# A last product split over two PSUM banks, and a copy moved behind an exponential

## The chip, the cores and the metric

The kernel runs on one core of one Trainium2 chip. The metric is the device time of one execution in microseconds. The core's engines are TensorE (PE; its weight loads are shown as PEld), VectorE (DVE), ScalarE (ACT), GpSimd (POOL) and SyncE (SP), and 16 DMA engines move data. Each engine runs its own instructions in order, and engines wait for each other by semaphores.

## The reference

Two layers are chained. The first is attention over 8 batches of 8 heads, 576 positions of 64 values each, with sparse masks: heads 0 to 3 are local (a position sees the 32 last ones up to itself), heads 4 to 7 are strided (a position sees the earlier ones with the same remainder by 32).

```
scores = scale * np.matmul(q, k.transpose(0, 1, 3, 2))
masks  = local for h < 4: 0 <= i - j < 32;  strided for h >= 4: j <= i and j % 32 == i % 32
attn   = softmax(where(masks, scores, -1e9))
x      = np.matmul(attn, v), heads side by side: 4608 tokens x 512
```

The second layer is a projection of the 4608 tokens to 2048 values, a leaky activation with a slope per column, and a projection back to 512:

```
h = x @ w_in
g = np.maximum(h, 0.0) + alpha * np.minimum(h, 0.0)
out = g @ w_out
```

Inputs and output are 32 bit floats; inside, the kernel uses 16 bit floats for the operands of matmuls.

## The kernel before

**The loop.** The tokens are cut into nine chunks of 512. The loop over n = 1 to 8 does chunk n's second layer in 30 steps: 16 steps of `lin1_piece` (L624 matmuls into a PSUM tile hps, ACT's `neg` at L636, DVE's combination into gT at L638) and 14 of `fast_piece`. `fast_piece` computes the projection back by a scheme of seven products of half-size blocks (P1, P4, P2, P6, P5, P7, P3, in this order), each in two halves of eight matmuls (L693). Their sums collect in four PSUM accumulators X, Y, Z and V: Y begins as a copy of X behind P1 (`seed`, L719), V as a copy of Y behind P6, and P3 adds onto V. DVE adds the accumulators onto output tiles (L644, through `sub`), and SP stores them.

**The attention in between.** Between these steps `attn_n` takes pieces of the attention of batch n + 1 from a list that was made ahead. A pair is two heads (four pairs to a batch, the last two strided), and a pair's work is one score piece (L411 matmuls, exponentials on ACT, masks on DVE), two or three pv pieces (L454 matmuls, L461 and L463 on DVE), and the turning of its result into xT, the input of `lin1_piece`. The score piece makes two halves. The first half's exponential (L424) and mask (L426) are issued at once. The second half's exponential is two instructions (L430), put into the list `defer`, and one is issued after each following step.

**The turning.** For batches from the third on, the first three pairs of a batch are turned by a DMA: `x_dma` issues it on SP. For the third pair, the first strided one, it writes a tile xs (L486), and ACT then copies xs into xT in token order (`x_copy`, L493, 128x576). The fourth pair is turned by eight transposes on TensorE into a PSUM tile xp (L471) and copied by ACT (L207). Of the list's iteration g, the score piece is that of pair g, the pv pieces those of pair g - 1, the transposes those of pair g - 2, and `x_copy` that of pair g - 3. So `x_copy` stands at the start of the next batch's second iteration, which is also where the loop over n goes on to its next chunk.

**PSUM.** Two pools of three one-bank tiles each: `phpool` (hps and the accumulators) and `pspool` (second halves of scores, pv, xp, and each third hps); a third pool holds the first half of the scores. A tile that is allocated again waits until the former one has been read.

**The end.** In the last chunk P3's two halves are added and stored apart, each 128 rows by 256 columns, so that the first store can start before the second half is done. Both halves lie in the same accumulator tile V:

Of the kernel before, what the change touches and what calls it, by code (L numbers as in the profile page):

```python
# [9 lines left out]
F32 = mybir.dt.float32  # L10
F16 = mybir.dt.float16
ALU = mybir.AluOpType
# [19 lines left out]
def kernel(  # L32
# [10 lines left out]
    nc = tc.nc  # L43
    keep = tc.keep_in_program_order
# [48 lines left out]
    pspool = ctx.enter_context(tc.tile_pool(name="ps", bufs=3, space=bass.MemoryType.PSUM))  # L93
    phpool = ctx.enter_context(tc.tile_pool(name="ph", bufs=3, space=bass.MemoryType.PSUM))
# [5 lines left out]
            name=nc.get_next_instruction_name(), act_func_set_id=6, ins=[], outs=[]  # L100
# [17 lines left out]
    DX = 2  # L118
# [184 lines left out]
    def turn_rows(b, nm):  # L303

        dst = qTs[0][:, :, 0:576] if nm == "q" else kTs[0][:, :, 32:608]
        for e in range(2):
            keep(nc.sync.dma_start_transpose(
                dst[:, e].rearrange("r (t p) -> r t p", p=96),
                rowed[(b, nm)][0:96, 768 * e : 768 * e + 768]))
# [187 lines left out]
    npair = 4 * B  # L497
    pairs = [make_pair(g) for g in range(npair)]
    pieces = []

    def feed(fn, g):
        pieces.append((g, fn))

    def T(u, nm):
        return lambda: transpose_piece(u, nm)

    def Pv(g, i):
        return lambda: pv_piece(pairs[g], i)

    def X(g):  # L510
        return lambda: x_piece(pairs[g])

    for g in range(7, npair + 2):
        c = g // 4
        a, p, t = g, g - 1, g + 1
        okA = 8 <= a < npair
        okP = 8 <= p < npair
        okT = 8 <= t < 4 * LX and t % 4 == 0
        nP = len(pairs[p].pgroups) if okP else 0
        seq = []  # L520
        if okA:
            seq.append(("S", lambda a=a: score_both(pairs[a])))
        if okP:
            seq.append(("P", Pv(p, 0)))
        if okT:
            seq.append(("T", T(t // 2, "q")))
        if 8 <= g - 2 < npair and not pairs[g - 2].xd:
            seq.append(("X", X(g - 2)))
        if okP:
            seq.append(("P", Pv(p, 1)))  # L530
        if okT:
            seq.append(("Tk", T(t // 2, "k")))
        if nP == 3:
            seq.append(("P", Pv(p, 2)))
        if not seq:
            seq.append(("N", lambda: None))

        todo = [(c, pr) for pr in range(2)] if g % 4 == 0 and 8 < g < npair else []

        if g % 4 == 1 and 9 <= g and c + 1 < B:  # L540
            todo = [(c + 1, nm) for nm in "qk"]
        lastP = max([i for i, z in enumerate(seq) if z[0] == "P"], default=len(seq) - 1)
        nslots = [i for i, z in enumerate(seq) if z[0][0] != "S"] or list(range(len(seq)))
        for i, (kind, fn) in enumerate(seq):
            extra = []
            if todo and i in nslots:
                left = len([z for z in nslots if z >= i])
                cnt = -(-len(todo) // max(1, left))
                extra = [todo.pop(0) for _ in range(min(cnt, len(todo)))]

            def run(fn=fn, extra=extra, g=g, c=c, kind=kind, lastp=(i == lastP), first=(i == 0)):
                fn()
                if first and g % 4 == 2 and LX <= c + 1 < B:
                    turn_rows(c + 1, "q")
                    turn_rows(c + 1, "k")
                for b, pr in extra:
                    if pr in ("q", "k"):
                        if b < LX:
                            cast_l(b, pr, "act")
                        if b + 1 < LX:  # L560
                            load_qk(b + 1, False, pr)
                        continue
                    cast_v(b, pr, "act" if b >= LX else "dve")
                    if pr == 1 and b + 1 < B:
                        load_v(b + 1, True)
                if kind == "Tk" and g % 4 == 3 and c + 3 < LX:
                    load_tail(c + 3, False)
                if lastp and g % 4 == 3 and LX <= c + 2 < B:
                    load_rows(c + 2, "q")
                    load_rows(c + 2, "k")  # L570
                if lastp:
                    if 4 * DX <= g - 1 < npair and pairs[g - 1].xd:
                        x_dma(pairs[g - 1])
                    if g % 4 == 3 and DX <= c + 1 < B:
                        over_v(c + 1, "sp")
                    if g % 4 == 3 and DX <= c + 1 < B:
                        transpose_d()
                    if g % 4 == 2 and DX <= c and c + 1 < B:
                        load_d(c + 1)
                    if g % 4 == 1 and DX < c and c + 1 < B:  # L580
                        load_v(c + 1, False)
                if first and 4 * DX <= g - 3 < npair and pairs[g - 3].xd and pairs[g - 3].strided:
                    x_copy(pairs[g - 3])
            feed(run, g - 2 if kind == "X" else -1)

    pos = {"i": 0}
# [56 lines left out]
    def sub(eng, o, x, y, op=ALU.subtract):  # L643
        keep(eng.tensor_tensor(o, x, y, op=op))  # L644
# [24 lines left out]
    cur = {}  # L669

    def fast_piece(n, i):

        name, tb = PRODUCTS[i // 2], i % 2
        last = n == NCH - 1
        g = gTs[n].rearrange("r (p j) t -> r j p t", j=2)
        w = wout16.rearrange("r (p j) c -> r j p c", j=2)
        st = sums["t"]
        lo, hi = slice(0, 256), slice(256, 512)
        bank, x, y = {
            "P1": ("X", g[:, 0, :, lo], w[:, 0, :, lo]),  # L680
            "P4": ("Z", g[:, 1, :, hi], wt[:, 2]),
            "P2": ("X", g[:, 1, :, lo], w[:, 1, :, lo]),
            "P6": ("Y", st[:, 1], wt[:, 1]),
            "P5": ("Z", st[:, 0], wt[:, 3]),
            "P7": ("Y", st[:, 2], wt[:, 0]),
            "P3": ("V", st[:, 3], w[:, 1, :, hi]),
        }[name]
        opens = name in ("P1", "P4", "P5")
        if name in ("P1", "P4") and tb == 0:
            cur[bank] = phpool.tile([128, 512], F32, tag="hps", name="f" + bank)  # L690
        z = cur[bank]
        for p in range(8):
            keep(nc.tensor.matmul(  # L693
                z[:, 256 * tb : 256 * tb + 256], x[:, p, 128 * tb : 128 * tb + 128], y[:, p],
                start=(opens and p == 0 and tb == 0), stop=(p == 7),
                skip_group_check=True))
        if last and name == "P3":
            h = slice(256 * tb, 256 * tb + 256)
            r0 = 512 * n + 128 * tb
            sub(nc.vector, cur["22"][:, h], z[:, h], cur["22"][:, h], ALU.add)  # L700
            keep(nc.sync.dma_start(out[r0 : r0 + 128, 256:512], cur["22"][:, h]))
            return
        if tb == 0:
            return

        def new(key):
            cur[key] = opool.tile([128, 512], F32, tag="osb", name="o" + key)
            return cur[key]

        def store(i, k, t):  # L710
            r0 = 512 * n + 256 * i
            keep(nc.sync.dma_start(
                out[r0 : r0 + 256, 256 * k : 256 * k + 256].rearrange("(b p) c -> p b c", p=128),
                t.rearrange("p (b c) -> p b c", c=256)))

        def seed(to, bank):

            cur[to] = phpool.tile([128, 512], F32, tag="hps", name="f" + to)
            keep(nc.scalar.copy(cur[to], bank))  # L719

        if name == "P1":
            seed("Y", z)
        elif name == "P4":
            keep(nc.scalar.copy(new("21"), z))
        elif name == "P2":
            keep(nc.scalar.copy(new("11"), z))
            store(0, 0, cur["11"])
        elif name == "P6":
            seed("V", z)
        elif name == "P5":  # L730
            keep(nc.scalar.copy(new("22"), z))
        elif name == "P7":
            sub(nc.vector, cur["21"], z, cur["21"], ALU.add)
            store(1, 0, cur["21"])
            sub(nc.vector, new("c22"), z, cur["22"], ALU.add)
            store(1, 1, cur["c22"])
        elif name == "P3":
            sub(nc.vector, cur["22"], z, cur["22"], ALU.add)
            store(0, 1, cur["22"])
# [218 lines left out]
```

## Time and profile before

| | |
|---|---|
| median of 3 runs | 307.68 us (306.0 to 307.92) |
| profiled execution | 306.29 us |
| its span in the profile | 304.5 us |
| TensorE busy | 291.3 us (96%) |
| DVE busy | 249.0 us (82%) |
| ACT busy | 188.6 us (62%) |
| POOL busy | 71.2 us (23%) |
| `x_copy` on ACT (L493) | 6 times, 1298 to 1307 ns, at 93.8, 125.0, 155.4, 185.7, 215.9 and 246.7 us |
| last DVE instruction starts | 301.31 us |
| granted TensorE clock | full, in all slices |

The span is what the profiler saw of the program, and the 1.8 us between it and the execution's time lie around it. Times in a timeline are microseconds from the start of the span. A row of a timeline merges instructions of one kind that follow each other: start, length, engine, line, operation, output and inputs, shapes, how many, and in brackets the idle time before it with what ended it. Matmuls overlap: each lasts some 270 ns from start to end, but the next one starts when the former's columns have streamed, after 0.109 us at 256 columns. In the list of waits, "A <- B: total, times, longest" says that A's engine stood idle until B released it; "issue" as a releaser means that the profile shows no releaser.

### The profile page before, as it was taken

The page shows a single profiled execution, that of the slowest core. Times are in us where ns is not written, and L with a number is a line of the kernel's source. Part 1 is how long each engine was busy: PE and PEld are TensorE (multiplying, and loading weights), DVE is VectorE, ACT ScalarE, POOL GpSimd, SP SyncE. Part 2 cuts the span into 40 slices and gives each one's busy share as a digit, 9 for nine tenths or more (in the row PEclk, how much of TensorE's full clock was granted, in tenths as well). Part 3 has the DMA queues.
Part 4 walks back from the last instruction along what each step waited for, and adds up shares of the span by engine and source line. Part 5 has one row for each costly group of instructions (what it writes and reads, how often), then busy time and mean ns, then how long its engine had stood idle before and what let it go on. Part 6 is the DMA issues. An engine that isn't in the chain of part 4 may idle for free. (4 is left out here: it accounts for less than half of the span.)

```text
span 304.5 us, 7136 instructions
## 1 busy us (share of the span) xinstructions
PE 291.3 (96%) x2841; PEld 196.2 (64%) x2841; DVE 249.0 (82%) x498; ACT 188.6 (62%) x343; POOL 71.2 (23%) x106
## 2 busy tenths in 40 slices
PE   6789988999999999999999999999999999999994
PEld 2554445554687468888874587458777964784583
DVE  4686879959988997889978997999799968937952
ACT  3665747389778767586568656865675456426630
POOL 9942274090312720353035201000000000000000
PEclk9999999999999999999999999999999999999999
DMA  7999999999999998999999999942810330012012
GB/s 218 226 214 207 205 193 204 173 175 184 245 126 234 138 136 44 159 199 153 111 163 185 152 102 181 174 78 42 195 46 1 77 105 2 0 41 99 0 37 103
DMA packets 95648, 40.56 MB, mean 133 GB/s; under 512 B 73904, under 2 KB 92608, under 8 KB 95616
## 3 DMA queue, kind: packets, MB, share of 16 engines
q0 software_dynamic: 49712, 18.36, 61.3%
q1 hardware_dynamic: 45632, 21.23, 37.0%
q10 hardware_dynamic: 272, 0.52, 0.6%
q8 instruction: 22, 0.36, 0.6%
q14 instruction: 10, 0.08, 0.1%
HBM read 36.83 MB, written 9.44 MB: 152 GB/s over the span
## 5 line engine op out<-in xcount | busy, mean ns | idle before, releaser
L624 PE MATMUL hps<-xT,win 128*128 128x512 f16 (+2 forms) x704 | 130.6, 340 | 0.3 <-DVE gT L638 0.3
L638 DVE SCALAR_TENSOR_TENSOR gT<-neg,oma,hps 128x512 f16<-128x512 f32 x144 | 102.9, 742 | 19.2 <-ACT neg L636 14.8
L636 ACT ACTIVATE neg<-hps 128x512 f32<-128x512 f32 x144 | 85.2, 598 | 44.3 <-PE hps L624 43.0
L624 PEld LDWEIGHTS <-win 128*128 128x128 f16 x704 | 63.6, 98 | 54.4 <-issue 0.6
L693 PEld LDWEIGHTS <-sg 128*128 128x128 f16 x512 | 47.3, 98 | 7.0 <-issue 1.3
L693 PEld LDWEIGHTS <-gT 128*128 128x128 f16 x384 | 35.2, 98 | 5.8 <-DVE gT L638 0.8
L463 DVE TENSOR_TENSOR x<-pv,rc 96x384 f16<-96x384 f32 (+2 forms) x62 | 33.0, 532 | 2.1
L693 PE MATMUL fY<-wt,sg 128*128 128x256 f16 x256 | 32.4, 273 | 0.0
L693 PE MATMUL fX<-wout,gT 128*128 128x256 f16 x256 | 31.7, 273 | 0.0
L454 PEld LDWEIGHTS <-et 72*128 72x128 f16 (+1 forms) x448 | 23.3, 98 | 8.8 <-DVE et L342 2.4
L644 DVE TENSOR_TENSOR sg<-gT 128x1024 f16<-128x1024 f16 x32 | 21.4, 681 | 0.0
L152 POOL DMA_DIRECT2D qsd<-in_q_dram x6 | 4.4, 730 | 67.8 <-DMA qT<-qsd 66.7
L430 ACT ACTIVATE et<-sph 128x288 f16<-128x288 f32 (+1 forms) x48 | 18.4, 409 | 0.0
L424 ACT ACTIVATE et<-sp 128x576 f16<-128x576 f32 (+1 forms) x24 | 15.5, 645 | 4.5 <-PE sp L411 4.5
L454 PE MATMUL pv<-vs,et 72*128 72x65 f16 x256 | 15.6, 194 | 1.9 <-DVE et L342 1.9
L693 PE MATMUL fV<-wout,sg 128*128 128x256 f16 x128 | 16.1, 272 | 1.1 <-DVE o L644 1.1
L693 PE MATMUL fZ<-wt,gT 128*128 128x256 f16 x128 | 16.3, 273 | 0.0
L693 PE MATMUL fZ<-wt,sg 128*128 128x256 f16 x128 | 16.0, 272 | 0.0
L765 PE MATMUL ops<-wout,gT 128*128 128x512 f16 x64 | 16.0, 379 | 0.0
L461 DVE RECIPROCAL rc<-pv 72x6 f32<-72x6 f32 (+2 forms) x80 | 14.6, 182 | 1.2 <-PE pv L454 1.0
L199 POOL DMA_DIRECT2D vl<-in_v_dram x9 | 10.4, 1157 | 19.0 <-PE xp L471 9.0
L426 DVE TENSOR_TENSOR et<-et,consts 128x576 f16<-128x576 f16 (+1 forms) x24 | 10.8, 452 | 4.7 <-ACT et L424 4.3
(105 smaller groups left out, 319.7 us busy)
## 6 DMA issues: line engine op xcount, KB each, us to landing
out_dram<-o SPq DMA_DIRECT2D x23, 256.0 KB, 2.8
stv<-in_v_dram POOLq DMA_DIRECT2D x8, 288.0 KB, 8.5
win<-in_moe_w_in_dram POOLq DMA_DIRECT2D x4, 512.0 KB, 10.7
wout<-in_moe_w_out_dram POOLq DMA_DIRECT2D x4, 512.0 KB, 17.9
out_dram<-oc SPq DMA_DIRECT2D x8, 256.0 KB, 3.3
vl<-in_v_dram POOLq DMA_DIRECT2D x7, 288.0 KB, 9.5
qsd<-in_q_dram POOLq DMA_DIRECT2D x6, 288.0 KB, 7.0
ksd<-in_k_dram POOLq DMA_DIRECT2D x6, 288.0 KB, 8.1
```

The costliest lines, as they stand in the source:

```text
L424: keep(nc.scalar.activation(ev.rearrange("r (y c) -> r y c", y=2), sp[0:r, :, 0:n], AF.Exp, scale=SCALE))
L426: keep(nc.vector.tensor_tensor(mv, mv, m, op=ALU.mult))
L430: keep(nc.scalar.activation(ev[:, n * y : n * y + n], sps[y][0:r, 0:n], AF.Exp, scale=SCALE))
L454: keep(nc.tensor.matmul(pv[:, 65 * x : 65 * x + 65], et[0:r, c : c + 128], v16[0:r, 2 * P.pr + hh, t, :] if P.strided else v16[:, 6 * (2 * ...
L461: keep(nc.vector.reciprocal(rc[0:w, 0:nb], pvv[:, :, 64]))
L463: keep(nc.vector.tensor_tensor(P.x16[0:w, c0 : c0 + 64 * nb].rearrange("r (c e) -> r c e", e=64), pvv[:, :, 0:64], rc[0:w, 0:nb].unsqueeze ...
L624: keep(nc.tensor.matmul(hps[:, dst : dst + w], win16[:, kk, 128 * m : 128 * m + 128], xT[:, kk, src : src + w], start=(kk == (0 if n else ...
L636: keep(nc.scalar.activation(neg, hps, AF.Relu, scale=-1.0))
L638: keep(nc.vector.scalar_tensor_tensor(gTs[n][:, m, :], neg, oma[:, m : m + 1], hps, op0=ALU.mult, op1=ALU.add))
L644: keep(eng.tensor_tensor(o, x, y, op=op))
L693: keep(nc.tensor.matmul(z[:, 256 * tb : 256 * tb + 256], x[:, p, 128 * tb : 128 * tb + 128], y[:, p], start=(opens and p == 0 and tb == 0) ...
L765: keep(nc.tensor.matmul(ops, gTs[n][:, kf, 128 * mt : 128 * mt + 128], wout16[:, kf, :], start=(kf == 0), stop=(kf == 15)))
```

## The change

It has two parts. In the list of attention pieces, `x_copy` is issued with the second piece of its iteration instead of the first (where the iteration has only one piece, still with that one). In the last chunk, the accumulator V is made of two tiles: V from `phpool` for P3's first half and V1 from `pspool` for its second; the one copy that seeds V becomes two copies of 256 columns.

```diff
-            def run(fn=fn, ..., first=(i == 0)):
+            def run(fn=fn, ..., first=(i == 0), at=i, seq=seq):
...
-                if first and 4 * DX <= g - 3 < npair and pairs[g - 3].xd and pairs[g - 3].strided:
+                if at == min(1, len(seq) - 1) and 4 * DX <= g - 3 < npair and pairs[g - 3].xd and pairs[g - 3].strided:
                     x_copy(pairs[g - 3])
...
         z = cur[bank]
+        zo = z[:, 256 * tb : 256 * tb + 256]
+        if last and name == "P3":
+            zo = cur["V1"][:, 0:256] if tb else z[:, 0:256]
         for p in range(8):
             keep(nc.tensor.matmul(
-                z[:, 256 * tb : 256 * tb + 256], x[:, p, 128 * tb : 128 * tb + 128], y[:, p],
+                zo, x[:, p, 128 * tb : 128 * tb + 128], y[:, p],
...
-            sub(nc.vector, cur["22"][:, h], z[:, h], cur["22"][:, h], ALU.add)
+            sub(nc.vector, cur["22"][:, h], zo, cur["22"][:, h], ALU.add)
...
+        elif name == "P6" and last:
+            cur["V"] = phpool.tile([128, 512], F32, tag="hps", name="fV")
+            cur["V1"] = pspool.tile([128, 512], F32, tag="ps", name="fV1")
+            keep(nc.scalar.copy(cur["V"][:, 0:256], z[:, 0:256]))
+            keep(nc.scalar.copy(cur["V1"][:, 0:256], z[:, 256:512]))
         elif name == "P6":
             seed("V", z)
```

## The prediction

> **What bounds the kernel now.** The page comes first: which engine is full, and when.
>
> ```profile
> PE 291.3 (96%) x2841; PEld 196.2 (64%) x2841; DVE 249.0 (82%) x498; ACT 188.6 (62%) x343; POOL 71.2 (23%) x106
> ...
> PE   6789988999999999999999999999999999999994
> ```
>
> TensorE works without a visible pause from the fourth slice to the last. So time comes off only where TensorE stands still, or behind its last matmul. The list of waits names one stall at the end (PE fV behind DVE o, 1.1 us, once) and one that recurs; this is the recurring one in the stretch from 100 to 240 us (total us, times, longest):
>
> ```profile
> PEld L471 <- issue: 1.0, 4, 0.3
> ```
>
> L471 are the eight transposes of the last strided pair of a batch. For the last stall I took the chain of work that ended last, in order of time (start, length, what):
>
> ```profile
> 299.76 0.43 DVE o L644
> 300.20 0.04 issue
> 300.24 1.05 PE fV L693 x8
> 301.29 0.02 issue
> 301.31 0.42 DVE o L644
> ```
>
> The reader is to see a handover, DVE to PE to DVE, with no overlap. For the recurring stall I took the timeline of one such place, first PE and then ACT (start, length, what, idle before):
>
> ```profile
> 155.71 0.35 PE L454 MATMUL pv<-vl,et 128*128 128x65 f16 x6
> 155.89 1.04 PE L693 MATMUL fV<-wout,sg 128*128 128x256 f16 x8
> 157.02 0.42 PE L471 MATMUL xp<-consts,x 72*128 72x72 f16 x8
> 157.28 1.04 PE L693 MATMUL fV<-wout,sg 128*128 128x256 f16 x8
> 158.15 0.59 PE L624 MATMUL hps<-xT,win 128*128 128x512 f16 x2
> ```
>
> ```profile
> 154.81 0.65 ACT L424 ACTIVATE et<-sp 128x576 f16<-128x576 f32 x1 [0.53 <-PE sp L411]
> 155.35 1.31 ACT L493 COPY xT<-xs 128x576 f16<-128x576 f16 x1
> 156.55 0.72 ACT L430 ACTIVATE et<-sph 128x288 f16<-128x288 f32 x2
> 157.48 0.64 ACT L207 COPY xT<-xp 128x576 f16<-128x576 f16 x1 [0.21 <-PE xp L471]
> ```
>
> Eight fV matmuls of 273 ns each span 1.04 us, so they start 0.109 us apart, and the ninth could start at 155.89 + 8 x 0.109 = 156.76. The transposes start at 157.02. They need a PSUM buffer of the pool of three that the first of the two L430 exponentials has to empty, and that one waits behind the 1.31 us copy until 156.55.
>
> **Part one, the copy of the turned strided result.** Nothing is added or removed; five of the six copies move (the sixth, at 246.7, belongs to a list with one piece and stays). In the changed instruction order ACT runs in four stages: exponential of sp, first L430, copy, second L430, copy of xp; in the first stage (94 us) both L430 and a 1.06 us cast of ql come ahead of the copy. So "behind both exponentials" holds for the one of sp and the first half of the other.
>
> What goes: in the four stages the first L430 ends near 155.35 + 0.41 = 155.8 (mean 0.41 by its rows), a microsecond before 156.76, so the transposes start at once. Worked the same way at each place: 126.62 - (125.52 + 0.87) = 0.23; 157.02 - 156.76 = 0.26; 187.32 - (186.19 + 0.87) = 0.26; 217.60 - (216.48 + 0.87) = 0.25. Together **0.99 us**, the 1.0 of the waits row. In the first stage pv starts at 96.15 = 94.41 + 16 x 0.109 and xp directly behind it: nothing to gain.
>
> What is late next: the second L430 runs about 156.9 to 157.3, not to 157.27, so as before; DVE's mask of it stood at 157.81 behind other DVE work, so it does not move. The copy of xp starts when the transposes end, 157.2 instead of 157.48. The changed program has one new wait, on TensorE: the third matmul of the next stage's first product (the contraction slice that the moved copy writes) waits for ACT in five stages. Queued behind it is all of TensorE. The copy ends near 155.7 + 1.3 = 157.0; TensorE comes there at 158.15 - 0.26 + 2 x 0.216 = 158.3, slack **1.3 us**. In the first stage ACT gives 93.83 + 0.30 + 0.31 + 0.96 + 1.30 = 96.7 and TensorE needs it at 96.59 + 0.43 = 97.0, slack **0.3 us**. A wait already met costs nothing visible: the two matmuls ahead of it already wait, for DMAs, and their starts are 0.216 us apart like all others. No DMA moves with the copy: the turning transfer was issued at 149.15 and lands in 2.7 to 4.2 us, before 154.
>
> Does the 0.26 us carry on? In the next stage DVE is 95% busy (14.18 of 15.00 us from 160 to 175) and TensorE even waits for it 0.06 to 0.12 us where the products start. But that DVE run starts at 160.50 after 1.45 us of idling for ACT's first neg, which waits 1.75 us for TensorE; the whole train starts earlier. I take all of 0.99; the bounds are 0 (absorbed) and 1.1 (with the small waits).
>
> **Part two, the end.** ACT's seed copy of 128x512, 0.57 us, becomes two of 128x256. No such row exists; from the rows 128x288 (0.41) and 128x576 (0.64) each lies between 0.29, half of 0.57, and 0.41, so 0.57 to 0.82 together. I take 0.7. ACT then frees fY at 295.6, while P7, which needs it, starts at 296.38 behind P5: P5 hides it; without that cover it would cost 0.1 to 0.25 us. The new bank comes from the pool of three, idle since the last first-product matmuls. What goes: the second fV group has no wait for DVE any more. It follows the first at 298.12 + 8 x 0.109 = 298.99 and ends at 300.0; the second DVE addition then follows the first at once, near 300.2 instead of 301.31, and its store can be issued at 300.67 instead of 301.76: **1.09 us** earlier.
>
> What is late next is the store. The DMA view from 299 to 304.5 us (slices of 0.1375 us):
>
> ```profile
> DMA  0000000699999999999983000059920000000000
> GB/s 0 0 0 0 0 0 0 216 343 328 305 365 350 335 335 350 357 357 321 350 328 127 0 0 0 0 194 357 313 90 0 0 0 0 0 0 0 0 0 0
> ...
> out_dram<-o SPq DMA_DIRECT2D x2, 128.0 KB, 1.9
> ```
>
> The three stores ahead keep all 16 engines full, near 340 GB/s, until 302.0; then half a microsecond of pause; then the last 131 KB, until 303.1. Issued earlier, the last store queues behind the others: 302.0 + 131 KB / 340 GB/s = 302.4 instead of 303.1, a gain of **0.7 us**, and 0.4 us of the 1.09 are lost. [...]
>
> **Sum.** 0.99 + 0.7 = 1.69 us off the span of 304.5, and nothing changes in the 1.8 us around it: 306.29 - 1.69 = **304.6** against the profiled execution. The four executions known are 306.0, 306.29, 307.68 and 307.92, two near 306.1 and two near 307.8, and their median as given is 307.68, 1.4 above the profiled one. Nothing says on which side the next falls, so I forecast from their mean 306.97: **305.3 us**, 0.55% less.
>
> **The rivals.**
> - The last store lands the whole 1.09 us earlier (engines not limiting it): 306.97 - 2.08 = 304.9. For it: the median time to landing of these stores, 1.9 us, is mostly not transfer; against: the full slices. 0.13.
> - The four stalls only move: DVE, 95% busy in the next stage, keeps its own pace and TensorE waits longer for gT where the products start. Then 0.7 is left: 306.3. For it the waits of 0.06 to 0.12 there, against it DVE's idle 1.45 us ahead. 0.17.
> - The change does not do what it says, because PE still meets a late seed or the additions stay serial: only 0.99 is left, 306.0. The changed program has no such wait. 0.05.
> - Slower: the moved copy ends after TensorE wants it at the new wait. From 1.3 us of lateness in four stages (0.3 in the first), each further microsecond stops TensorE a microsecond; 0.33 us past these points in five stages eats the 1.69, and 1.0 past them in all five gives 306.97 + 5.0 - 1.69 = 310.3. Against it: the copies last 1298 to 1307 ns in all six rows and their transfers have long landed. 0.08.
>
> My own forecast holds the rest, 0.57.
>
> **The numbers.** What a measurement here can tell is about 1%, 3.1 us. No case but the slow one leaves that band; the scatter of the executions themselves, 1.9 us between lowest and highest, can push a gain of 0.55 to 0.7% over it. Faster 0.13, within 0.81, slower 0.06. The range: low from the lowest execution with the full gain, 306.0 - 2.1 = 303.9; high from the highest with the tail alone, 307.92 - 0.7 = 307.2.
>
> **What would show it.** The waits lose "PE fV behind DVE o" (1.1) and L471's row falls from 1.0 to near nothing; L624 gets no wait for ACT; the second fV group stands 0.1 us behind the first one's last start; the DMA pause before the last store is gone and the slices run full without a break; the span is near 302.8. It would be wrong if a new wait of PE for ACT xT appears, if gT waits at the products grow by 0.2 us a stage, or if other stages (before 94 us, where nothing moves) differ by more than all this.

## The result and the profile after

The changed kernel takes 304.94 us (median of 20 runs, 304.14 to 309.29); the kernel before, run beside it, takes 307.8 us (median of 20, 305.8 to 310.07). The ratio is 0.9928, with a 95% interval of 0.99 to 0.9955: faster, by less than 1%. The forecast was 305.3. (The ratio leaves out the slow run of 309.29 us and is not that of the two medians, 0.991.)

The profiled execution of this comparison is that of 309.29 us, in which TensorE waits 2.5 us for a DMA, so the lines below are from a second profile of the same kernel (306.58 us, span 304.8).

In the chain of work that ended last, the handover from DVE to PE to DVE is gone (start, length, what):

```profile
300.64 0.09 issue
300.74 0.42 DVE o L644
301.16 0.33 DVEq L961
```

The two additions stand in one row of the timeline of the end (start, length, engine, line), and TensorE's sixteen matmuls of the last product in one group without a pause:

```profile
299.10 1.91 PE L696 MATMUL fV<-wout,sg 128*128 128x256 f16 x16
...
300.74 0.76 DVE L644 TENSOR_TENSOR o<-fV,o 128x256 f32<-128x256 f32 x2
301.22 0.86 SPq L704 DMA_DIRECT2D out_dram<-o  x2
```

In the middle, the place that the prediction showed, first PE and then ACT:

```profile
157.60 1.04 PE L696 MATMUL fV<-wout,sg 128*128 128x256 f16 x8
158.48 0.42 PE L471 MATMUL xp<-consts,x 72*128 72x72 f16 x8
158.74 1.04 PE L696 MATMUL fV<-wout,sg 128*128 128x256 f16 x8
159.61 0.59 PE L624 MATMUL hps<-xT,win 128*128 128x512 f16 x2
```

```profile
156.52 0.65 ACT L424 ACTIVATE et<-sp 128x576 f16<-128x576 f32 x1 [0.53 <-PE sp L411]
157.06 0.41 ACT L430 ACTIVATE et<-sph 128x288 f16<-128x288 f32 x1
157.35 1.31 ACT L493 COPY xT<-xs 128x576 f16<-128x576 f16 x1
158.55 0.42 ACT L430 ACTIVATE et<-sph 128x288 f16<-128x288 f32 x1
158.94 0.64 ACT L207 COPY xT<-xp 128x576 f16<-128x576 f16 x1
```

The transposes start 0.88 us behind the fV group's start, eight times 0.109 us, where they started 1.13 us behind it. The copy ends at 158.66; TensorE's third matmul of the next chunk is due at 159.61 + 0.43 = 160.04. In the stretch from 100 to 240 us L471 has no row in the list of waits any more, and from 94 us on no wait of PE above the list's bound is left at all.

How long each stage takes can be read without the start of the execution, which scatters: from the first P1 matmul of one chunk to that of the next, in us, and at last to the landing of the last store. The first column holds the first copy that moves, the sixth the one that does not.

| chunk to chunk | 1-2 | 2-3 | 3-4 | 4-5 | 5-6 | 6-7 | 7-8 | 8 to last landing |
|---|---|---|---|---|---|---|---|---|
| before | 32.03 | 31.31 | 30.24 | 30.29 | 29.98 | 27.84 | 26.06 | 15.84 |
| both parts | 32.02 | 31.08 | 29.98 | 30.05 | 29.74 | 27.84 | 26.06 | 15.15 |
| difference | 0.01 | 0.23 | 0.26 | 0.24 | 0.24 | 0 | 0 | 0.69 |

That is 0.98 us in the middle and 0.69 us at the end, 1.67 us in all, 0.55% of the span.

### The profile page after: what moved, and what is told of

Its sections match the earlier page's. It is cut to its first block, busy times and chain, and to the rows that moved or that the text cites. A ratio compares the mean times of both kernels' runs of the same rounds, so it can differ in the third digit from the quotient of the medians.

```text
span 307.5 us, 7136 instructions
## 1 busy us (share of the span) xinstructions
PE 292.7 (95%) x2841; PEld 197.3 (64%) x2841; DVE 249.0 (81%) x498; ACT 188.8 (61%) x344; POOL 70.9 (23%) x106
## 5 line engine op out<-in xcount | busy, mean ns | idle before, releaser
L430 ACT ACTIVATE et<-sph 128x288 f16<-128x288 f32 (+1 forms) x48 | 18.8, 409 | 0.0
L773 PE MATMUL ops<-wout,gT 128*128 128x512 f16 x64 | 16.8, 394 | 0.0
```

The costliest lines, as they stand in the source:

```text
L430: keep(nc.scalar.activation(ev[:, n * y : n * y + n], sps[y][0:r, 0:n], AF.Exp, scale=SCALE))
L773: keep(nc.tensor.matmul(ops, gTs[n][:, kf, 128 * mt : 128 * mt + 128], wout16[:, kf, :], start=(kf == 0), stop=(kf == 15)))
```

## The experiments

### Both parts once more, and each alone

Both parts are the changed kernel, unedited:

> Both parts, as changed. My account (0.99 us from four stalls of the transposes, 0.7 us from the end): 1.7 us less than before, ratio 0.9945; the transposes follow the fV matmuls without a gap, the last store lands 0.3 to 0.4 us behind the one ahead of it. If the last store moved by its whole 1.09 us: 2.1 us, ratio 0.993, and no more than 0.1 us between the two landings. If the stalls only moved: 0.7 us, ratio 0.998, and waits for gT where the products start grow by 0.2 us in each of four stages.

The copy alone is the kernel before with this edit:

```diff
-                if first and 4 * DX <= g - 3 < npair and ...
+                if at == min(1, len(seq) - 1) and 4 * DX <= g - 3 < npair and ...
```

> The copy of the turned result moved, the end left as it was. My account: 1.0 us less, ratio 0.997; the four stalls gone, the second group of the last product still 1.1 us behind DVE. If the stalls only moved into the next stage: no difference, ratio 1.000, with longer waits for gT. Both ratios differ by about the width of an interval, so the rows of the trace decide: distance between the ends of corresponding stages.

The bank alone is the changed kernel with that line put back:

> The end changed, the copy left where it was. My account: 0.7 us less, ratio 0.998; last addition about 1.1 us earlier after the first half's, last landing 0.7 us earlier. With a store that moves whole: 1.1 us, ratio 0.9965. The four stalls of 0.23 to 0.26 us ahead of the transposes stay.

| | median | ratio to before, 95% interval | stages 2-3 to 5-6 | 8 to last landing |
|---|---|---|---|---|
| both | 304.88 | 0.9916 (0.9882 to 0.995) | 31.08, 29.98, 30.05, 29.74 | 15.15 |
| copy alone | 306.55 | 0.9963 (0.9929 to 0.9997) | 31.09, 30.43, 30.04, 29.74 | 15.84 |
| bank alone | 307.05 | 0.9987 (0.996 to 1.0013) | 31.32, 30.23, 30.29, 29.99 | 15.15 |

The parts add up, and each stays in its place: the copy gives the four stages and nothing at the end, the bank gives the end and nothing in the stages. (The 30.43 holds a wait of 0.45 us for a DMA, told of below; without it the stage is 29.98.) The rival in which the stalls only move is refuted: the stages are shorter by the whole stall, and the weight loads' waits for gT where the products start are the same, here from 100 to 240 us in the kernel before and then with both parts (total us, times, longest):

```profile
PEld L693 <- DVE gT L638: 0.8, 4, 0.2
```

```profile
PEld L696 <- DVE gT L638: 0.8, 4, 0.2
```

With the bank alone the recurring stall is still there, as the waits from 100 to 240 us of that kernel show:

```profile
PEld L471 <- issue: 1.1, 4, 0.3
```

### The copy later still

The copy was moved one piece further, behind the transposes' piece. It meets the condition of the slow rival:

```diff
-                if at == min(1, len(seq) - 1) and 4 * DX <= g - 3 < npair and ...
+                if at == min(2, len(seq) - 1) and 4 * DX <= g - 3 < npair and ...
```

> Both parts, but the copy is issued with the third piece, behind both second-half exponentials and the copy of xp. The slow rival's mechanism with its condition met: by my numbers ACT ends the copy near 159.05 where TensorE wants it at 158.3, a stall of 0.8 us in each of four stages and of some 1.7 us in the first (copy ends 98.7, wanted at 97.0): 4.9 us slower than with both parts, so 3.2 us slower than before, ratio 1.010, with a wait of PE hps L624 for ACT xT. If TensorE's new wait were no real limit (it could use the time otherwise, or the copy is not needed that early): the same time as with both parts, ratio 0.9945.

314.36 us (median of four runs, 309.62 to 314.9), ratio 1.014. Its interval, 1.0064 to 1.0216, rests on two of the four runs, so that the traces say more than the times. The list of waits of this kernel from 94 us on (total us, times, longest), and the stage near 166 us in its timeline:

```profile
PE hps L624 <- ACT xT L493: 4.7, 5, 2.4
```

```profile
165.70 0.59 PE L624 MATMUL hps<-xT,win 128*128 128x512 f16 x2
166.92 1.89 PE L624 MATMUL hps<-xT,win 128*128 128x512 f16 x8 [0.62 <-ACT xT L493]
```

Two matmuls run and the third waits, where the prediction put it. The stages are 36.30, 31.79, 30.77, 30.83 and 30.37 us; against both parts that is 4.28 and then 0.71, 0.79, 0.78 and 0.63. Four times 0.8 was expected, and 0.73 is the mean. So the mechanism of the slow rival is real, and the changed kernel is clear of it by its place, by some 1.3 us in those stages.

In the first stage 1.7 us were expected and 4.28 came. ACT's timeline there shows what I left out: this late, a second cast (kl) stands ahead of the copy too.

```profile
99.85 0.64 ACT L207 COPY xT<-xp 128x576 f16<-128x576 f16 x1 [1.32 <-PE xp L471]
100.39 1.05 ACT L207 CAST kl<-kl 128x1024 f16<-128x1024 f32 x1
101.33 1.30 ACT L493 COPY xT<-xs 128x576 f16<-128x576 f16 x1
```

That makes a pause of 2.6 us on TensorE. The other 1.7 us come behind it, in busy time by stretch (us, then busy us of each engine, granted clock, DMA share, GB/s):

```profile
99.90:103.30 3.40, 0.96 (x5) 0.36 (x4) 1.06 (x3) 2.74 (x3) 1.84 (x3) 1.00 1.11 328
103.30:106.70 3.40, 3.40 (x15) 1.44 (x14) 1.41 (x2) 1.24 (x3) 3.40 (x6) 0.51 1.00 111
```

TensorE was busy for 0.96 of 3.4 us, and for the next 3.4 us its clock was granted by half: the matmuls of 512 columns start 0.427 us apart instead of 0.216. So this pause cost 4.3 us, nearly twice its own time. Not every pause of that length does. In the profile of 309.29 us of the changed kernel TensorE waited as long near 157 us:

```profile
PE pv L454 <- DMA vl<-vl: 2.5, 1, 2.5
```

Its clock stayed full behind that, and the stage took 32.66 us instead of 29.98, the pause and no more. The late copy's own run of 309.62 us has a mean granted clock of 0.994, where the other three have 0.987 to 0.989; a second stretch at half clock may be what it lacks, but no profile of it was taken.

### The last store's queue

To see whether the last store is held up by the two stores ahead of the halves, these were left out; 256 rows of the output are then not written.

```diff
-            store(1, 0, cur["21"])
+            if not last:
+                store(1, 0, cur["21"])
             sub(nc.vector, new("c22"), z, cur["22"], ALU.add)
-            store(1, 1, cur["c22"])
+            if not last:
+                store(1, 1, cur["c22"])
```

> Both parts, and in the last chunk the two 256 KB stores ahead of the halves (o21 and c22) are left out, so those 256 rows of the output are not written. If the 0.4 us that the last store did not gain are the queue on the DMA engines: it lands 1.7 us after its issue as it did before the change, 0.35 us earlier relative to the start of the last chunk's first product than with both parts (14.8 instead of 15.15 us). If its time to landing is fixed otherwise: no change, 15.15 us and 2.07 us.

In one execution, from the last chunk's P1 to the last landing it takes 14.85 us. The DMA views of both parts (slices of 0.13 us from 299.9) and of this kernel (0.125 us from 298):

```profile
DMA  0000000049999999999999989950000000000000
...
out_dram<-o SPq DMA_DIRECT2D x2, 128.0 KB, 2.1
```

```profile
DMA  0000000000000000000079848992000000000000
...
out_dram<-o SPq DMA_DIRECT2D x2, 128.0 KB, 1.8
```

With both parts the slices are full without a break, where before there was half a microsecond of pause; the two halves then land 2.1 us after their issue (the last one 2.06), and 1.8 us with the two stores left out (the last one 1.79). The 0.3 us are most of the expected 0.35: the store was held up by the stores ahead and not by a fixed time.

### P7's halves apart

If the queue is the limit, the stores ahead must leave sooner. Y was put into two banks as V was, in the last chunk alone, and P7's halves are added and stored apart:

```diff
+        if last and name in ("P6", "P7", "P3"):
+            zo = cur[bank + "1"][:, 0:256] if tb else z[:, 0:256]
...
+        if last and name == "P7":
+            ...
+            sub(nc.vector, cur["21"][:, h], zo, cur["21"][:, h], ALU.add)
+            keep(nc.sync.dma_start(out[r0 : r0 + 128, 0:256], cur["21"][:, h]))
+            sub(nc.vector, cur["c22"][:, h], zo, cur["22"][:, h], ALU.add)
+            keep(nc.sync.dma_start(out[r0 : r0 + 128, 256:512], cur["c22"][:, h]))
+            return
```

> Both parts, and in the last chunk Y too lies in two banks, so that P7's halves are added and stored apart, each as soon as its eight matmuls are done. By the queue account the first stores leave near 10.3 us after the start of the last chunk's first product instead of 11.5, the engines are free again when the last one is issued, and it lands at 14.6 to 14.7 us instead of 15.15: 0.5 us, 0.2% better than both parts, within the interval of the times. If the fixed time to landing or DVE's chain is the limit: 15.1 us or later, since DVE has two instructions more.

The first store leaves 10.33 us and the last one lands 14.59 us after the start of the last chunk's first product, 0.56 us sooner than 15.15, as expected. All six stores of the end land 1.7 to 1.8 us after their issue. But the span ends 1.37 us behind the last landing, where it ended 1.05 us behind it: 0.25 us are left. The times can't show that: 306.4 us, ratio 0.9967 (0.9935 to 1.0), beside both parts in the same comparison:

> Both parts as changed, beside the two kernels above on one chip: ratio to before 0.992 to 0.995; from the start of the last chunk's first product to the last landing 15.15 us.

306.5 us, ratio 0.9969 (0.9934 to 1.0004), the stages 32.02, 31.09, 29.98, 30.04 and 29.74 us and the end 15.16 us, as in the lines above. So the ratio lies outside what was expected of it (0.992 to 0.995) while every stage repeats.

### The copy of v's overlap

In the copy-alone profile TensorE waited 0.45 us near 157 us for a copy from SBUF to SBUF that SP issues (L226, the rows of v that neighbouring blocks share), and in the first profile of the changed kernel 2.5 us. L226 was issued ahead of the turning transfer instead of behind it, on top of the kernel with P7 apart:

> As the one with P7's halves apart, and SP issues the copy of the overlapping v rows ahead of the turning transfer instead of behind it. In two of six profiles TensorE waited for that copy in the stage near 157 us (0.45 and 2.5 us). If those were the copy's place in SP's queue: it is issued 1.3 us or more earlier, no such wait is left, and the median falls by up to half a microsecond below that with P7 apart. If they come from a start that is late or from busy engines: waits of that kind can still turn up and the median is the same. The copy of xs is then 1 us later, covered by 2 us or more.

305.64 us, ratio 0.9953 (0.9924 to 0.9982), an interval that overlaps those of the two others. The rows of L226, with both parts and then with the new order:

```profile
DMA to landing us min/median/max: 2.2/3.7/6.6
```

```profile
DMA to landing us min/median/max: 3.9/7.0/11.2
```

SP issues it 2 to 8 us sooner at five of its six places, and it takes longer to land, so that only part of the head start is left. Counted from the start of a chunk's first product it lands 3.3 to 4.8 us sooner at three of the five: near 157 us at 8.1 instead of 11.4 us, which leaves 4.4 us instead of 1.1 until TensorE reads it. At the two others it lands 0.2 us sooner: in the stage near 188 us at 187.60, 0.45 us before TensorE read it, and with both parts at 187.06, 0.29 us before. So an earlier place in SP's queue gives room where TensorE had waited, though not everywhere, and the times are too scattered to show a gain. It is not the whole cause: in the two profiles with a wait the copy was issued 7.2 us behind the start of the product, as in those without, and took 5.7 and 7.9 us to land, where in the others it took 2.2 to 4.9. That this is the load on the engines is likely, but it was not tried apart.

### The two groups of times

With both parts alone the times of one comparison lie at 303.64 to 304.35 and 306.3 to 308.17 us, with nothing between; in the first comparison they lie at 304.14 to 305.74 and 306.54 to 309.29. Seven of the ten profiles taken to this point have a stretch of half clock near 47 us, in the part that the change does not touch, and an example stands in the stretches of both parts' third comparison:

```profile
45.00:48.40 3.40, 1.37 (x24) 1.03 (x23) 1.63 (x4) 3.29 (x6) 2.19 (x3) 1.00 1.91 146
48.40:51.80 3.40, 3.40 (x33) 1.86 (x31) 2.45 (x7) 1.72 (x5) 1.59 (x3) 0.50 1.19 229
```

Ahead of it TensorE waits some 2 us for a mask. Six matmuls of zeros were put into that pause:

```diff
         pv = pspool.tile([128, 512], F32, tag="ps", name="pv")
+        if P.g == 6 and a == 0:
+            for _ in range(6):
+                keep(nc.tensor.matmul(pv, wrm[:, 0:128], wrm, start=True, stop=True, ...))
```

> Both parts, and six matmuls of zeros (1.3 us) into the tile of the first strided pv piece of the second batch, ahead of its own matmuls, where TensorE stands still near 46 us for 0.8 to 2.5 us in every profile. In seven of ten profiles the granted clock is half for 3.4 us straight behind that pause, and the times of one kernel lie in two groups some 2 us apart. If the pause brings the half clock: no such stretch near 47 us, nearly all runs in the lower group, median near 304.3, ratio to before 0.988 to 0.992. If the groups come from elsewhere: as many runs in the upper group as with both parts alone, median 304.9 to 306.5, and up to 1 us is lost where the pause is shorter than the filling.

> All that helped or did no harm: both parts, P7's halves apart, v's overlap copy ahead of the turning transfer, and the six filling matmuls. If each is worth what the traces show (1.7 us, 0.25 us at the end of the span, nothing, and 1.7 us in the runs with the half clock): median near 304.0, ratio to before 0.986 to 0.991. If the filling does nothing: as the kernel without it, 0.995.

> Both parts as changed, beside the two kernels above on one chip: ratio to before 0.992 to 0.997, runs in two groups near 304.3 and 306.5.

| one comparison | median | lowest to highest | ratio to before, 95% interval |
|---|---|---|---|
| both, filled | 305.29 | 304.59 to 306.21 | 0.9935 (0.9911 to 0.9958) |
| both, P7 apart, L226 ahead, filled | 304.72 | 304.44 to 305.16 | 0.9921 (0.9891 to 0.9952) |
| both | 305.44 | 304.02 to 308.1 | 0.9943 (0.9907 to 0.9978) |

The filling does what the first account says to the upper group: none of 19 runs is above 306.21, where six of twelve with both parts alone are at 306.26 to 308.1. Neither filled profile has the half clock near 47 us. Of the profiles of both parts alone, all four (306.58, 306.49, 306.87 and 309.29 us) fell in the upper group and have it. The wait for the mask is gone in the first filled profile and 0.3 us in the second. Over all 13 profiles, the first P1 matmul starts at 79.7 to 80.4 us in the five without that half clock and at 81.7 to 82.9 us in the eight with it.

What stays open is what a run of the lower group is. In the four comparisons with both parts alone, all 22 runs above 306.2 us have a mean granted clock of 0.992 to 0.994, and all 18 runs with 0.997 or more took at most 305.74 us. But eleven more runs with 0.993 or 0.994 took 303.86 to 304.88 us. So a half clock somewhere does not by itself put a run into the upper group: the first filled profile has it at 9.0 us, and its first P1 starts at 80.35 us all the same. No profile of a lower run with both parts alone was taken. Nor does the filling reach what was expected of it: the ratios are 0.9935 for 0.988 to 0.992, and 0.9921 for 0.986 to 0.991. The lower group with both parts alone starts at 304.02, the filled ones at 304.4 to 304.6. That is half a microsecond that the filling may itself cost; it was not resolved. The version with everything has the lowest median of its comparison and the narrowest scatter (in seven runs), but its interval overlaps that of both parts.

## Why the prediction was right

**The recurring stall, 0.99 us.** The stages are shorter by 0.23, 0.26, 0.24 and 0.24 us, for 0.23, 0.26, 0.26 and 0.25 in the sum. The step that the first L430 frees the transposes' buffer is borne out by both its sides: the stall leaves with the copy's move and stays without it. The trace of the kernel before shows the step itself: near 157 us the first L430 ends at 156.97 us and the second at 157.27, and the transposes start at 157.02, right behind the first.

**That it carries on.** It does, in full. DVE's share of 95% in the next stage is no limit here, where its run starts from an idle DVE (1.45 us of idling ahead of it, in the kernel before); it shifts with TensorE.

**The new wait and its slack.** From 94 us on, no wait of TensorE for ACT is in the changed kernel's profile. In the stage near 160 us the copy ends 1.38 us before TensorE needs it, for 1.3 in the prediction; in the first stage it ends at 98.61 and TensorE needs it at 98.53 + 0.43 = 98.96, 0.35 us for 0.3. The price of the slow rival, a microsecond of TensorE for each one of lateness, was right in four stages (0.73 for 0.8 us a stage). In the first stage of the kernel with the late copy 4.28 us came for 1.7: a cast that I left out, and a clock that was halved behind the pause. Whether a pause of 1 us, as in that rival, would bring the clock down too is not shown; the four pauses of 0.6 to 0.8 us did not.

**The seed copies.** Each half takes 0.36 us (357 and 365 ns) and both end 0.63 us after the first starts, inside the bounds of 0.57 to 0.82 and under the cover of P5.

**The end, 0.7 us.** It is 0.69. The issue of the last store moved by 1.05 us, from 14.13 to 13.08 us behind the start of the last chunk's first product, and not by 1.09: when the second addition ends, at 301.50, SP is still issuing the first half's store (the two issues take 0.86 us from 301.22 on). The landing moved by 0.69. Of the 0.36 us between the two the removed stores give 0.3 back, so most of it is the queue. If the time to landing were the same whatever is ahead, as in the rival of the whole 1.09 us, the landing would have moved with the issue. It did not, and where nothing was ahead these stores, which SP issues, landed within 1.7 to 1.8 us, their bytes included (the last one 1.71 us in the kernel before, 1.79 us with the two stores left out).

**The span and the part before 94 us.** The prediction named a span near 302.8 us as a sign, and a difference before 94 us of more than its whole gain as a sign of being wrong. The second profile of the changed kernel has a span of 304.8 us, and its first P1 matmul starts at 81.82 us, where it started at 79.88 before: 1.94 us later, in the part that the change does not touch, and more than the 1.69. So this sign did appear, and no comparison of whole spans can show the gain. What shows it is the rest: from that matmul to the end of the span it is 222.97 us instead of 224.64, 1.67 less, the two parts alone give the same stages, and those that the change leaves alone are equal to 0.01 us. The late start goes with the half clock near 47 us, which the profile before does not have.

**The median.** The traces give 1.67 us, a ratio of 1 - 1.67 / 304.5 = 0.9945, which the intervals of all four comparisons of the changed kernel hold. Their medians differ by 2.86, 3.05, 0.01 and 2.19 us. What the prediction could not size was its base: it noted two groups of executions, did not know what made them, and took their mean. A median moves by some 1.5 us with the share of runs in the upper group, in either kernel (304.88 to 306.5 with both parts, 306.51 to 307.93 before). So the sum was right, but that the forecast of 305.3 lies only 0.36 from the median is in part luck: the median of the kernel before came out 0.8 above the 306.97 that was taken, and the difference of 2.86 us is 1.2 more than the sum.

## What to carry to other kernels

A small stall that returns at the same place is worth following to the buffer it waits for: here a copy that nobody needed for another microsecond stood on ACT ahead of the exponential that freed a bank, and moving it one piece later was enough, while two pieces later made it the limit. At the end of a kernel ask of each store not when it is issued but how many bytes are ahead of it, at the rate that the DMA slices show (here near 340 GB/s). (Even so, sooner landings are not all gain: of the 0.56 us that P7's halves apart gave the last landing, the span kept 0.25.) And where the gain is smaller than the scatter of the executions, compare the lengths of stages between fixed instructions in the traces: they mostly repeated to 0.01 us here, when medians moved by 1.5.

## What the runs showed of the hardware that I had not expected

Half the clock can follow a pause on TensorE of 1.6 to 2.5 us: so long was its wait for the mask in the eight profiles that have the half clock near 47 us. This half clock lasted 3.4 us in each of them (3.413 us in that of 309.29 us). It began 41.0 us behind the clock's rise to full (5.75 us into the span in that profile) in seven of them, twelve times 3.41 us, and 44.4 us behind it, thirteen times, in the kernel with the late copy; the one at 103.3 us there began 51.2 us behind the next rise, fifteen times. In the 3.41 us ahead of these nine, TensorE (matmuls and weight loads together) was busy for 0.97 to 1.79 us. In the three unfilled profiles without it, the pause of 0.8 to 2.2 us near 46 us fell across two such stretches or was short, and neither stretch was busy for less than 2.28 us. The busy share does not decide it alone: the stretch with the 2.5 us wait for a DMA near 157 us was busy for 1.71 us and no half clock followed, and the first stretch behind the clock's rise is busy for 1.6 to 2.7 us, while only one of thirteen profiles has a half clock behind it (at 9.0 us, behind 1.67 us). All nine starts thus lie on whole multiples of the half clock's own length. Which executions are hit may hang on where such a stretch falls; that is my estimate, from these nine starts and the three unfilled profiles without one.

The end of a program is not a fixed time either. From the last landing to the end of the span it took 1.04 to 1.05 us in the kernel before and with both parts, 1.17 us with two stores left out, and 1.36 to 1.37 us where P7's halves are stored one by one. What sets it was not tried; more stores are not the whole answer, since fewer lengthened it too.
